# First loads from two queues, first half units over six PSUM banks, statistics spread

## The chip, the cores and the metric

The kernel runs on one core of one Trainium2 chip. The metric is the time of one execution on the device in microseconds; where several runs are given, their median.

## The reference

```python
def reference(A_x, A_w_r, A_w_i, B_x, B_w_gate, B_w_up, B_w_down):
    def _A_ref(x, w_r, w_i):
        X = rfft2(x.astype(float32), axes=(-2, -1))
        X = X * (w_r + 1j * w_i)
        return irfft2(X, s=(S, D), axes=(-2, -1)).astype(bfloat16)

    def _B_ref(x, w_gate, w_up, w_down):
        g = jnp.einsum("bsd,df->bsf", x, w_gate)
        u = jnp.einsum("bsd,df->bsf", x, w_up)
        h = _gelu(g) * u
        return jnp.einsum("bsf,fd->bsd", h, w_down)

    x = A_x
    xn = _layernorm(x, axis=-1)
    return x + _A_ref(xn, A_w_r, A_w_i) + _B_ref(xn, B_w_gate, B_w_up, B_w_down)
```

`x` is 1 x 2048 x 512, the weights of the gated part are 512 x 1792 (gate and up) and 1792 x 512 (down), all in bfloat16. The row x is normalized, goes through a spectral filter (a two-dimensional Fourier transform, a product, and back) and through a gated feed-forward layer, and the three are added.

## The kernel before, in words

The 2048 rows are 16 tiles `j` of 128 rows (row 16p + j is on partition p of tile j), and four blocks `b` of four tiles. Everything is issued in an order that is written out by hand from L699 on. `_Sched` keeps a list of instructions for each engine; an engine runs its list strictly in order and waits, before an instruction, on the semaphores of what it depends on. `_Ring` hands out PSUM banks in turn: the next user of a bank waits for the bank's last readers. Before the change there are three rings: three banks for the gate and up products (`ps_gu`), four for transposes and the spectral part (`ps_sp`), one for the down product (`ps_dn`).

Loads: ACT's queue issues `small` at L345, 224 KB that hold the identity (the first 128 columns), BM and CM. SP's queue issues all the rest in the order of L347 to L373: x tiles 0 to 3 one by one, the first piece of the gate and up weights (columns 0 to 255, called w0 here), the second piece (256 to 767, w1), x tiles 4 to 7, the third piece w2, x tiles 8 to 15, w3, the constants `fa` of the spectral part, the down weights `wd`. The pieces are cut by `WPIECES`, and a piece counts as loaded when both its transfers, gate and up, are there.

The start, L699 to L723: 18 warm-up matmuls on zeros run on the matmul engine (PE). DVE takes mean and variance of tiles 0 and 1 (`ln_stats`: L399 and L400), ACT a square root (L405), DVE a reciprocal (L409) and the normalized rows (`ln_apply`, L422). PE transposes them (L440): four transposes into each of two banks, copied to `xnT` by DVE (L446) and by ACT (L448). Then come six half units on the first 256 rows of block 0, one for each of six chunks `fc` of 128 weight columns. A half unit (`geglu_unit`) is four matmuls for the gate (from `wg_sb`) and four for up (`wu_sb`), all L495, 256 columns wide; ACT applies gelu (L507) and DVE multiplies into `hT` (L515). Chunks 0 and 1 need w0, chunks 2 to 5 need w1. Ahead of chunk 2, DVE normalizes tiles 2 and 3, whose statistics it took after the first copies, with the reciprocal root from GpSimd (POOL, `ln_rstd`, L414 and L415). After the six half units tiles 2 and 3 are transposed, and six more half units do the second 256 rows. In DVE's list the statistics of tiles 4 and 5 stand ahead of the first of these, those of tiles 6 and 7 ahead of the second.

From L746 on the units are full, 512 columns wide, beginning with chunk 6 of block 0. After it, DVE normalizes tiles 4 to 7, POOL starts the folds of the spectral part (L460, L461), one more unit follows, and tiles 4 to 7 are transposed (16 transposes). From there on the spectral part's stages (L567, L583, L614, L635, L661, L681) and the full and down units (L543) alternate on PE until the last four down units, which end the kernel.

Of the kernel before, what the change touches and what calls it, by code (L numbers as in the profile page):

```python
# [209 lines left out]

class _Ring:

    def __init__(self, nslots):
        self.n = nslots
        self.pos = 0
        self.readers = [[] for _ in range(nslots)]

    def alloc(self, n=1):
        while self.pos % n != 0:
            self.pos += 1  # L220
        base = self.pos % self.n
        self.pos += n
        deps = []
        for s in range(base, base + n):
            deps.extend(self.readers[s])
            self.readers[s] = []
        return base, deps
# [8 lines left out]
def bass_parallel_sum__spectral_gfnet__glu_gated_geglu__prompt_kernel(  # L236
# [21 lines left out]
    with ExitStack() as es:  # L258
# [49 lines left out]
        EM = eg[:, 0:NJ * P].rearrange("p (j q) -> p j q", j=NJ)  # L308
        G = eg[:, NJ * P:].rearrange("p (r k) -> p r k", r=4)

        ps_gu = es.enter_context(nc.psum_tensor("ps_gu", [P, 3 * 512], F32))
        ps_sp = es.enter_context(nc.psum_tensor("ps_sp", [P, 4 * 512], F32))
        ps_dn = es.enter_context(nc.psum_tensor("ps_dn", [P, 512], F32))
        ps_sp_bf = ps_sp[:, :].bitcast(BF16)

        def gu_bank(slot):
            return ps_gu[:, slot * 512:(slot + 1) * 512]

        def sp_bank(slot):
            return ps_sp[:, slot * 512:(slot + 1) * 512]  # L320

        def sp_pair(slot):
            return ps_sp[:, slot * 512:(slot + 2) * 512].rearrange("p (a c) -> p a c", a=2)[:, :, 0:NK]

        def sp_bank_bf(slot):
            return ps_sp_bf[:, slot * 1024:(slot + 1) * 1024]

        ring_gu = _Ring(3)
        ring_sp = _Ring(4)
        ring_dn = _Ring(1)  # L330

        streams = [("pe", 1), ("act", 1), ("dve", 1), ("pool", 1)]
        streams += [(n, 16) for n in ("x0", "x1", "x2", "x3", "xc1", "xc2", "xc3", "small", "fa", "eg", "wd", "wr", "wi",
                                      "w0", "w1", "w2", "w3", "dr0", "dr1", "perm1", "perm2_0", "perm2_1", "out")]
        for name, inc in streams:
            sem = es.enter_context(nc.semaphore("sem_" + name))
# [5 lines left out]
            return total(stream)  # L342


        ev_small = load("small", small[:], c_small.ap(), eng="act")  # L345
        ev_x = {}
        for j in range(4):  # L347
            ev_x[j] = load("x%d" % j, x_sb[:, j, :], xv[:, j, :])
# [2 lines left out]
        ev_w = {}  # L351
        spec = {}

        def load_w(i):
            a, b = WPIECES[i]
            for dst, src in ((wg_sb, B_w_gate), (wu_sb, B_w_up)):
                load("w%d" % i, dst[:, :, a:b], src[:, a:b].rearrange("(r p) f -> p r f", p=P))
            ev_w[i] = total("w%d" % i)

        def load_xc(m):  # L360
# [1 line left out]
            for j in range(4 * m, 4 * m + 4):  # L362
                ev_x[j] = ev

        load_w(0)
        load_w(1)
        load_xc(1)
        load_w(2)
        load_xc(2)
        load_xc(3)  # L370
        load_w(3)
        ev_fa = load("fa", fa[:], c_fa.ap())
        ev_wd = load("wd", wd_sb[:], wdv)  # L373
        d1 = nc.dram_tensor("stage_p", [NJ, P, 512], BF16).ap()
# [50 lines left out]
        ev_xnT = {}  # L425
        tr = {}

        def transposes(a, b):

            n = (b - a) * P  # L430
            evs = []
            for h in range(2):
                slot, bdeps = ring_sp.alloc(1)
                bank = sp_bank_bf(slot)[:, 0:2 * n].rearrange("p (r s) -> p r s", r=2)

                def f_tr(e, h=h, bank=bank):
                    ins = None
                    for r in range(2):
                        for j in range(a, b):
                            ins = e.transpose(bank[:, r, (j - a) * P:(j - a + 1) * P], xn[:, j, (2 * h + r) * P:(2 * h + r + 1) * P], ident)  # L440
                    return ins

                ev_t = sch.op("pe", f_tr, deps=[ev_small] + [ev_xn[j] for j in range(a, b)] + bdeps)
                dst = xnT[:, 2 * h:2 * h + 2, a * P:b * P]
                if h == 0:
                    ev = sch.op("dve", lambda e, dst=dst, bank=bank: e.tensor_copy(dst, bank), deps=[ev_t])  # L446
                else:
                    ev = sch.op("act", lambda e, dst=dst, bank=bank: e.activation(dst, bank, ACT.Copy), deps=[ev_t])  # L448
                ring_sp.add_reader(slot, ev)
                evs.append(ev)  # L450
            for j in range(a, b):
                ev_xnT[j] = evs
                tr[j] = ev_t
# [16 lines left out]
        def warm_up():  # L470

            ev = sch.op("dve", lambda e: e.memset(hT[1][:, 0, :], 0.0))

            def f(e):
                ins = None
                for i in range(NWARM):
                    ins = e.matmul(ps_dn[:, :], hT[1][:, 0, 0:P], hT[1][:, 0, :], start=True, stop=True)
                return ins

            hT_readers[1].append(sch.op("pe", f, deps=[ev]))  # L480

        def geglu_unit(b, fc, a=0, w=512):

            k = geg["k"]
            geg["k"] = k + 1
            s2 = k % NGG
            hb = b % 2
            evw = [ev_w[i] for i, (lo, hi) in enumerate(WPIECES) if lo < (fc + 1) * P and fc * P < hi]
            evx = [ev_xnT[4 * b + i] for i in range(a // P, (a + w) // P)]
            gslot, gdeps = ring_gu.alloc(1)  # L490

            def mm(e, wsb, slot, dcs=range(NDC)):
                ins = None
                for dc in dcs:
                    ins = e.matmul(gu_bank(slot)[:, 0:w], wsb[:, dc, fc * P:(fc + 1) * P], xnT[:, dc, b * 512 + a:b * 512 + a + w],  # L495
                                   start=(dc == 0), stop=(dc == NDC - 1))
                return ins

            if b == 0 and fc == 0:
                sch.op("pe", lambda e: mm(e, wg_sb, gslot, (0, 1)), deps=evw + [x[0] for x in evx] + gdeps)  # L500
                ev_gm = sch.op("pe", lambda e: mm(e, wg_sb, gslot, (2, 3)), deps=[x[1] for x in evx])
            else:
                ev_gm = sch.op("pe", lambda e: mm(e, wg_sb, gslot), deps=evw + evx + gdeps)
            uslot, udeps = ring_gu.alloc(1)
            ev_um = sch.op("pe", lambda e: mm(e, wu_sb, uslot), deps=udeps)
            gg = gg_sb[s2][:, 0:w]
            ev_gg = sch.op("act", lambda e: e.activation(gg, gu_bank(gslot)[:, 0:w], ACT.Gelu_apprx_tanh),  # L507
                           deps=[ev_gm] + gg_readers[s2])
            gg_readers[s2] = []
            ring_gu.add_reader(gslot, ev_gg)  # L510
            hdeps = []
            if fc == 0 and a == 0:
                hdeps = list(hT_readers[hb])
                hT_readers[hb] = []
            ev_h = sch.op("dve", lambda e: e.tensor_tensor(hT[hb][:, fc, a:a + w], gu_bank(uslot)[:, 0:w], gg, ALU.mult),  # L515
                          deps=[ev_um, ev_gg] + hdeps)
            ring_gu.add_reader(uslot, ev_h)
            gg_readers[s2].append(ev_h)
            ev_h_block.setdefault(b, []).append(ev_h)

# [8 lines left out]
        def down_unit(b, jj):  # L529
            hb = b % 2  # L530
            j = 4 * b + jj

            ring, bank = (ring_gu, gu_bank) if b == 3 else (ring_dn, lambda slot: ps_dn[:, :])
            parts = 2 if j == NJ - 1 else 1
            w = D // parts
            for h in range(parts):
# [168 lines left out]
        ln_recip(0, 2, ev_sq)  # L705
        ln_apply(0)
        ln_apply(1)
        transposes(0, 2)
        ln_stats(2)
        ln_stats(3)  # L710
        ln_rstd(2, 4)
        for fc in range(NHALF):
            if fc == 2:
                ln_apply(2)
                ln_apply(3)
            geglu_unit(0, fc, 0, 256)
        transposes(2, 4)
        for fc in range(NHALF):
            if fc in (0, 1):
                ln_stats(4 + 2 * fc)  # L720
                ln_stats(5 + 2 * fc)
            geglu_unit(0, fc, 256, 256)
        ln_rstd(4, 8)  # L723
        fillers = []
        for b in range(4):
# [22 lines left out]
            ln_apply(j)  # L748
        folds(0, [ev_xn[7]])
        filler()  # L750
        transposes(4, 8)
        folds(1)
        filler()
        for m in range(2, NDC + 2):
            for i in range(4):
                j = 4 * (m - 2) + i
                if m < NDC:
                    if i < 2:
                        ln_stats(4 * m + 2 * i)
                        ln_stats(4 * m + 2 * i + 1)  # L760
                    else:
                        ln_apply(4 * m + 2 * i - 4)
                        ln_apply(4 * m + 2 * i - 3)
                    if i == 1:
                        ln_rstd(4 * m, 4 * m + 4)
                filler()
                unit_d(j)
                if j >= 1:
                    unit_A(j - 1)
                if j == 1:  # L770
                    load_filter("wr", wr_sb, A_w_r)
                if j == 5:
                    load_filter("wi", wi_sb, A_w_i)
                if j == 9:
                    shuffle(0)
            if m < NDC:
                transposes(4 * m, 4 * m + 4)
                folds(m)
        filler()
        unit_A(NJ - 1)  # L780
# [70 lines left out]
```

## Time and profile before

| what | value |
|---|---|
| median of 3 runs | 196.79 us (196.22 to 196.89) |
| the profiled execution | 197.14 us, its span 195.4 us |
| busy share of the span | PE 96%, weight loads 53%, DVE 49%, ACT 46%, POOL 21% |
| chain that ended last | PE 89%, DVE 4%, DMA 4%, SP's queue 2% |
| read from HBM, written | 15.71 MB, 4.19 MB |
| DMA issues at the start, KB each, us from issue to landing | x tiles 0 to 3: 128.0, 3.5 (median); w0 gate: 256.0, 4.4; w0 up: 256.0, 5.5; small: 224.0, 3.0 |

The profile is one execution taken by the hardware profiler. The span runs from its first instruction to its last, so the execution's own time lies a little above it. An arrow in a line names what ended the idle time before an instruction. "PEld" is the weight load of the matmul engine, which overlaps matmuls.

### The profile page before, as it was taken

What the parts mean: (1) busy time and instruction counts of PE and PEld (TensorE: products, weight loads), DVE (VectorE), ACT (ScalarE), POOL (GpSimd) and SP (SyncE); (2) the same over time, 40 slices, a digit from 0 to 9 for tenths busy, and PEclk for the clock granted to TensorE, in tenths of its full rate; (3) what the DMA queues carried; (4) which work ended last, traced back from release to release, by engine and by line L of the source; (5) the groups of instructions that cost most, each with busy time, mean ns of one, the idle gap of its engine ahead of it and who ended that gap; (6) DMA issues with size and microseconds to landing.
All of it is one profiled execution on the core that took longest, in us unless ns stands there. A gap on an engine that the chain in (4) does not pass through costs nothing.

```text
span 195.4 us, 3030 instructions
## 1 busy us (share of the span) xinstructions
PE 187.5 (96%) x1120; PEld 103.8 (53%) x1120; DVE 95.2 (49%) x200; ACT 90.6 (46%) x167; POOL 40.2 (21%) x38
## 2 busy tenths in 40 slices
PE   7878999999999999999999999999999999999995
PEld 2465645555555554445555555544555555554453
DVE  2758469595322122445555455514454646465221
ACT  2534344776747462237546563633443635365000
POOL 0010259464530000000000000000134424444200
PEclk9999999999999999999999999999999999999999
DMA  4999950599996742900112111110001111110011
GB/s 143 323 370 375 374 185 2 128 182 198 253 197 154 207 142 83 325 25 18 51 46 56 49 50 51 48 51 20 2 27 61 50 54 43 41 54 0 11 46 54
DMA packets 25294, 22.20 MB, mean 114 GB/s; under 512 B 1472, under 2 KB 24512, under 8 KB 25152
## 3 DMA queue, kind: packets, MB, share of 16 engines
q1 hardware_dynamic: 25136, 21.78, 40.2%
q10 hardware_dynamic: 144, 0.23, 0.5%
q8 instruction: 9, 0.15, 0.3%
q14 instruction: 5, 0.04, 0.1%
HBM read 15.71 MB, written 4.19 MB: 102 GB/s over the span
## 4 chain that ended last, share of the span: by engine, by line
PE 89%; DVE 4%; DMA 4%; SPq 2%; issue 1%; ACT 0%; DVEq 0%
PE ps_gu L495 46%; PE ps_dn L543 19%; PE ps_gu L543 6%; DMA wu_sb<-in_B_w_up_dram 4%; PE ps_sp L567 4%; PE ps_sp L681 3%; PE ps_sp L661 2%; PE ps_sp L614 2%; PE ps_sp L636 2%; PE ps_sp L635 2%; PE ps_sp L583 2%; SPq L341 2%; PE ps_sp L440 1%; DVE hT L515 1%; DVE st L399 1%; DVE bufA L422 1%
## 5 line engine op out<-in xcount | busy, mean ns | idle before, releaser
L495 PE MATMUL ps_gu<-xnT,wg_sb 128*128 128x512 bf16 (+1 forms) x248 | 58.6, 358 | 3.3 <-DMA wu_sb<-in_B_w_up_dram 1.1
L495 PE MATMUL ps_gu<-xnT,wu_sb 128*128 128x512 bf16 (+1 forms) x248 | 58.5, 358 | 0.0
L515 DVE TENSOR_TENSOR hT<-ps_gu,gg 128x512 bf16<-128x512 f32 (+1 forms) x62 | 39.4, 637 | 35.0 <-PE ps_gu L495 34.3
L507 ACT ACTIVATE gg<-ps_gu 128x512 bf16<-128x512 f32 (+1 forms) x62 | 34.5, 557 | 27.9 <-PE ps_gu L495 27.8
L693 POOL TENSOR_TENSOR x_sb<-x_sb,bufC 128x512 bf16<-128x512 bf16 x16 | 18.4, 1151 | 108.8 <-DVE bufC L688 108.8
L543 PE MATMUL ps_dn<-wd_sb,hT 128*128 128x512 bf16 x168 | 38.2, 379 | 0.0
L495 PEld LDWEIGHTS ps_gu<-xnT,wu_sb 128*128 128x128 bf16 x248 | 24.3, 98 | 24.2
L495 PEld LDWEIGHTS ps_gu<-xnT,wg_sb 128*128 128x128 bf16 x248 | 23.5, 98 | 20.8 <-DMA wu_sb<-in_B_w_up_dram 2.4
L543 PEld LDWEIGHTS ps_dn<-wd_sb,hT 128*128 128x128 bf16 x168 | 16.4, 98 | 17.9
L549 DVE TENSOR_TENSOR x_sb<-ps_dn,x_sb 128x512 bf16<-128x512 f32 x12 | 8.3, 692 | 23.2 <-PE ps_dn L543 23.2
L575 ACT ACTIVATE X<-ps_sp 128x512 bf16<-128x512 f32 x16 | 11.9, 745 | 14.8 <-PE ps_sp L567 14.8
L641 ACT ACTIVATE Vp<-ps_sp 128x514 bf16<-128x514 f32 x16 | 9.6, 599 | 18.3 <-PE ps_sp L636 9.6
L666 ACT ACTIVATE bufA<-ps_sp 128x512 bf16<-128x512 f32 x16 | 9.6, 597 | 17.1 <-PE ps_sp L661 17.1
L622 DVE TENSOR_TENSOR M<-Xc,wr_sb 128x514 bf16<-128x514 bf16 x16 | 6.9, 428 | 14.7 <-ACT Xc L619 14.7
L543 PE MATMUL ps_gu<-wd_sb,hT 128*128 128x512 bf16 (+1 forms) x70 | 12.3, 337 | 0.3 <-DVE hT L515 0.3
L399 DVE BATCH_NORM_STATS2 st<-x_sb 128x6 f32<-128x512 bf16 x16 | 10.7, 672 | 2.6 <-DMA x_sb<-in_A_x_dram 2.6
L460 POOL TENSOR_TENSOR bufB<-xnT 128x1024 bf16<-128x1024 bf16 x4 | 8.5, 2124 | 15.0 <-DVE bufA L422 5.6
L619 ACT ACTIVATE Xc<-ps_sp 128x514 bf16<-128x514 f32 x16 | 9.5, 595 | 4.0 <-PE ps_sp L614 4.0
L686 DVE TENSOR_TENSOR bufC<-ps_sp,bufC 128x256 bf16<-128x256 f32 x16 | 6.8, 424 | 6.7 <-ACT bufC L685 6.7
L543 PEld LDWEIGHTS ps_gu<-wd_sb,hT 128*128 128x128 bf16 x70 | 6.8, 98 | 5.9 <-DVE hT L515 0.6
L681 PE MATMUL ps_sp<-fa,bufA 128*128 128x256 bf16 x64 | 9.6, 273 | 0.0
L567 PE MATMUL ps_sp<-fa,bufB 128*128 128x256 bf16 x64 | 9.6, 272 | 0.0
(42 smaller groups left out, 142.9 us busy)
## 6 DMA issues: line engine op xcount, KB each, us to landing
stage_p<-bufA SPq DMA_DIRECT2D x16, 128.0 KB, 5.2
bufC<-stage_p SPq DMA_DIRECT2D x4, 512.0 KB, 5.2
bufB<-Vp SPq DMA_DIRECT2D x64, 32.0 KB
out_dram<-x_sb SPq DMA_DIRECT2D x15, 128.0 KB, 1.8
wd_sb<-in_B_w_down_dram SPq DMA_DIRECT2D x1, 1792.0 KB, 14.4
wr_sb<-in_A_w_r_dram SPq DMA_DIRECT2D x6, 257.0 KB, 5.2
wi_sb<-in_A_w_i_dram SPq DMA_DIRECT2D x6, 257.0 KB, 8.0
wg_sb<-in_B_w_gate_dram SPq DMA_DIRECT2D x3, 512.0 KB, 7.7
```

The lines of the kernel that those rows point to most:

```text
L399: ev = sch.op("dve", lambda e: e.bn_stats(st[:, j, :], x_sb[:, j, :]), deps=[ev_x[j]])
L495: ins = e.matmul(gu_bank(slot)[:, 0:w], wsb[:, dc, fc * P:(fc + 1) * P], xnT[:, dc, b * 512 + a:b * 512 + a + w], start=(dc == 0), stop=(d ...
L507: ev_gg = sch.op("act", lambda e: e.activation(gg, gu_bank(gslot)[:, 0:w], ACT.Gelu_apprx_tanh), deps=[ev_gm] + gg_readers[s2])
L515: ev_h = sch.op("dve", lambda e: e.tensor_tensor(hT[hb][:, fc, a:a + w], gu_bank(uslot)[:, 0:w], gg, ALU.mult), deps=[ev_um, ev_gg] + hdeps)
L543: ins = e.matmul(bank(slot)[:, 0:w], hT[hb][:, fc, jj * P:(jj + 1) * P], wd_sb[:, fc, cs], start=(fc == 0), stop=(fc == NFC - 1))
L567: ins = e.matmul(bank, fold[:, r, j * P:(j + 1) * P], FD[:, r, :], start=(r % 2 == 0), stop=(r % 2 == 1))
L575: ev_X1[j] = sch.op("act", lambda e: e.activation(dst, src, ACT.Copy), deps=[ev_p, X1_readers[j % NX1]])
L619: ev_c = sch.op("act", lambda e: e.activation(Xc[s2][:], sp_pair(slot), ACT.Copy), deps=[ev_p] + Xc_readers[s2])
L641: ev_v = sch.op("act", lambda e: e.activation(Vp[s2][:], sp_pair(slot), ACT.Copy), deps=[ev_p] + Vp_readers[s2])
L666: ev_ZT[j] = sch.op("act", lambda e: e.activation(ZT[:, :, j, :], src, ACT.Copy), deps=[ev_p] + [spec["dr%d" % q] for q in range(2)])
L681: ins = e.matmul(bank[:, h:h + HD], ZT[:, ci, j, :], G[:, ci, :], start=(ci < 2), stop=(ci >= 2))
L693: ev_o = sch.op("pool", lambda e: e.tensor_tensor(x_sb[:, j, :], x_sb[:, j, :], rS[s2], ALU.add), deps=[a, b, ev_xn[j]] + ev_acc.get(j, []))
```

## The change

1. ACT's queue issues the identity alone (32 KB, a semaphore of its own), and behind it the two transfers of w0. SP's queue goes from the x tiles straight to w1. The rest of `small` is loaded by SP behind w3, ahead of `fa`.
2. The eight PSUM banks become one tensor with one list of readers, and a ring is a tuple of bank numbers. The three old rings keep their banks (0 to 2, 3 to 6, 7). Two new ones share them: `ring_first`, six banks (0, 1, 2, 7, 5, 6) for the twelve half units, and `ring_tr`, banks 3 and 4, for the transposes of tiles 2 and 3 and of tiles 4 to 7.
3. The first transposes (tiles 0 and 1) go to four banks, two transposes each (`per=1`), and four copies, by DVE and ACT in turn. The first half unit's four gate matmuls wait each for its own copy.
4. The transposes of tiles 2 and 3 move from behind the sixth half unit to behind the fourth.
5. The statistics of tiles 4 to 7 come one at a time, behind the first four half units of the second 256 rows, not two at a time ahead of the first two.

```diff
 class _Ring:
-    def __init__(self, nslots):
-        self.n = nslots
+    def __init__(self, banks, readers):
+        self.banks = banks
         self.pos = 0
-        self.readers = [[] for _ in range(nslots)]
+        self.readers = readers
     def alloc(self, n=1):
-        while self.pos % n != 0:
-            self.pos += 1
-        base = self.pos % self.n
+        self.pos = -(-self.pos // n) * n
+        base = self.banks[self.pos % len(self.banks)]
...
+        bank_readers = [[] for _ in range(8)]
+        ring_gu = _Ring((0, 1, 2), bank_readers)
+        ring_sp = _Ring((3, 4, 5, 6), bank_readers)
+        ring_dn = _Ring((7,), bank_readers)
+        ring_first = _Ring((0, 1, 2, 7, 5, 6), bank_readers)
+        ring_tr = _Ring((3, 4), bank_readers)
...
-        ev_small = load("small", small[:], c_small.ap(), eng="act")
+        ev_id = load("ident", small[:, 0:P], c_small.ap()[:, 0:P], eng="act")
...
-        load_w(0)
+        load_w(0, eng="act")
         load_w(1)
...
         load_w(3)
+        ev_small = load("small", small[:, P:], c_small.ap()[:, P:])
         ev_fa = load("fa", fa[:], c_fa.ap())
...
-        def transposes(a, b):
+        def transposes(a, b, ring, per=2):
...
-            for h in range(2):
-                slot, bdeps = ring_sp.alloc(1)
+            for h in range(NDC // per):
+                slot, bdeps = ring.alloc(1)
...
-                if h == 0:
+                if h % 2 == 0:
                     ev = sch.op("dve", lambda e, dst=dst, bank=bank: e.tensor_copy(dst, bank), deps=[ev_t])
                 else:
                     ev = sch.op("act", lambda e, dst=dst, bank=bank: e.activation(dst, bank, ACT.Copy), deps=[ev_t])
...
-            if b == 0 and fc == 0:
-                sch.op("pe", lambda e: mm(e, wg_sb, gslot, (0, 1)), deps=evw + [x[0] for x in evx] + gdeps)
-                ev_gm = sch.op("pe", lambda e: mm(e, wg_sb, gslot, (2, 3)), deps=[x[1] for x in evx])
+            if b == 0 and fc == 0 and a == 0:
+                for dc in range(NDC):
+                    ev_gm = sch.op("pe", lambda e, dc=dc: mm(e, wg_sb, gslot, (dc,)), deps=evw + [x[dc] for x in evx] + gdeps)
...
-        transposes(0, 2)
+        transposes(0, 2, ring_sp, 1)
         ln_stats(2)
         ln_stats(3)
         ln_rstd(2, 4)
         for fc in range(NHALF):
-            if fc == 2:
+            geglu_unit(0, fc, 0, 256, ring_first)
+            if fc == 1:
                 ln_apply(2)
                 ln_apply(3)
-            geglu_unit(0, fc, 0, 256)
-        transposes(2, 4)
+            if fc == 3:
+                transposes(2, 4, ring_tr)
         for fc in range(NHALF):
-            if fc in (0, 1):
-                ln_stats(4 + 2 * fc)
-                ln_stats(5 + 2 * fc)
-            geglu_unit(0, fc, 256, 256)
+            geglu_unit(0, fc, 256, 256, ring_first)
+            if fc < 4:
+                ln_stats(4 + fc)
         ln_rstd(4, 8)
...
-        transposes(4, 8)
+        transposes(4, 8, ring_tr)
```

More of the change, by code (lines that the diff above doesn't have):

```diff
@@ L309, in bass_parallel_sum__spectral_gfnet__glu_gated_geglu__prompt_kernel, with bank_of @@
         G = eg[:, NJ * P:].rearrange("p (r k) -> p r k", r=4)
[L311 to L320, printed above, removed]
+        ps = es.enter_context(nc.psum_tensor("ps", [P, 8 * 512], F32))
+        ps_bf = ps[:, :].bitcast(BF16)
+        def bank_of(slot):
+            return ps[:, slot * 512:(slot + 1) * 512]
+        gu_bank = sp_bank = bank_of
         def sp_pair(slot):
-            return ps_sp[:, slot * 512:(slot + 2) * 512].rearrange("p (a c) -> p a c", a=2)[:, :, 0:NK]
+            return ps[:, slot * 512:(slot + 2) * 512].rearrange("p (a c) -> p a c", a=2)[:, :, 0:NK]
         def sp_bank_bf(slot):
[L326 to L330, printed above, removed]
+            return ps_bf[:, slot * 1024:(slot + 1) * 1024]
+        bank_readers = [[] for _ in range(8)]
[4 more added lines that the diff above has]
+        ring_tr = _Ring((3, 4), bank_readers)
         streams = [("pe", 1), ("act", 1), ("dve", 1), ("pool", 1)]
-        streams += [(n, 16) for n in ("x0", "x1", "x2", "x3", "xc1", "xc2", "xc3", "small", "fa", "eg", "wd", "wr", "wi",
+        streams += [(n, 16) for n in ("x0", "x1", "x2", "x3", "xc1", "xc2", "xc3", "ident", "small", "fa", "eg", "wd", "wr", "wi",
                                       "w0", "w1", "w2", "w3", "dr0", "dr1", "perm1", "perm2_0", "perm2_1", "out")]
@@ L352, in bass_parallel_sum__spectral_gfnet__glu_gated_geglu__prompt_kernel, with load_w @@
         spec = {}
-        def load_w(i):
+        def load_w(i, eng="sp"):
             a, b = WPIECES[i]
             for dst, src in ((wg_sb, B_w_gate), (wu_sb, B_w_up)):
-                load("w%d" % i, dst[:, :, a:b], src[:, a:b].rearrange("(r p) f -> p r f", p=P))
+                load("w%d" % i, dst[:, :, a:b], src[:, a:b].rearrange("(r p) f -> p r f", p=P), eng=eng)
             ev_w[i] = total("w%d" % i)
@@ L426, in bass_parallel_sum__spectral_gfnet__glu_gated_geglu__prompt_kernel @@
         tr = {}
-        def transposes(a, b):
+        def transposes(a, b, ring, per=2):
             n = (b - a) * P
             evs = []
-            for h in range(2):
-                slot, bdeps = ring_sp.alloc(1)
-                bank = sp_bank_bf(slot)[:, 0:2 * n].rearrange("p (r s) -> p r s", r=2)
+            for h in range(NDC // per):
+                slot, bdeps = ring.alloc(1)
+                bank = sp_bank_bf(slot)[:, 0:per * n].rearrange("p (r s) -> p r s", r=per)
                 def f_tr(e, h=h, bank=bank):
                     ins = None
-                    for r in range(2):
+                    for r in range(per):
                         for j in range(a, b):
-                            ins = e.transpose(bank[:, r, (j - a) * P:(j - a + 1) * P], xn[:, j, (2 * h + r) * P:(2 * h + r + 1) * P], ident)
-                    return ins
-                ev_t = sch.op("pe", f_tr, deps=[ev_small] + [ev_xn[j] for j in range(a, b)] + bdeps)
-                dst = xnT[:, 2 * h:2 * h + 2, a * P:b * P]
-                if h == 0:
+                            ins = e.transpose(bank[:, r, (j - a) * P:(j - a + 1) * P],
+                                              xn[:, j, (per * h + r) * P:(per * h + r + 1) * P], ident)
+                    return ins
+                ev_t = sch.op("pe", f_tr, deps=[ev_id] + [ev_xn[j] for j in range(a, b)] + bdeps)
+                dst = xnT[:, per * h:per * h + per, a * P:b * P]
+                if h % 2 == 0:
                     ev = sch.op("dve", lambda e, dst=dst, bank=bank: e.tensor_copy(dst, bank), deps=[ev_t])
@@ L448, in transposes @@
                     ev = sch.op("act", lambda e, dst=dst, bank=bank: e.activation(dst, bank, ACT.Copy), deps=[ev_t])
-                ring_sp.add_reader(slot, ev)
+                ring.add_reader(slot, ev)
                 evs.append(ev)
@@ L476, in f, with geglu_unit @@
                 for i in range(NWARM):
-                    ins = e.matmul(ps_dn[:, :], hT[1][:, 0, 0:P], hT[1][:, 0, :], start=True, stop=True)
+                    ins = e.matmul(bank_of(7), hT[1][:, 0, 0:P], hT[1][:, 0, :], start=True, stop=True)
                 return ins
             hT_readers[1].append(sch.op("pe", f, deps=[ev]))
-        def geglu_unit(b, fc, a=0, w=512):
+        def geglu_unit(b, fc, a=0, w=512, ring=None):
             k = geg["k"]
@@ L487, in geglu_unit @@
             hb = b % 2
+            ring = ring or ring_gu
             evw = [ev_w[i] for i, (lo, hi) in enumerate(WPIECES) if lo < (fc + 1) * P and fc * P < hi]
             evx = [ev_xnT[4 * b + i] for i in range(a // P, (a + w) // P)]
-            gslot, gdeps = ring_gu.alloc(1)
+            gslot, gdeps = ring.alloc(1)
             def mm(e, wsb, slot, dcs=range(NDC)):
@@ L497, in mm @@
                 return ins
-            if b == 0 and fc == 0:
-                sch.op("pe", lambda e: mm(e, wg_sb, gslot, (0, 1)), deps=evw + [x[0] for x in evx] + gdeps)
-                ev_gm = sch.op("pe", lambda e: mm(e, wg_sb, gslot, (2, 3)), deps=[x[1] for x in evx])
+            if b == 0 and fc == 0 and a == 0:
+                for dc in range(NDC):
+                    ev_gm = sch.op("pe", lambda e, dc=dc: mm(e, wg_sb, gslot, (dc,)), deps=evw + [x[dc] for x in evx] + gdeps)
             else:
                 ev_gm = sch.op("pe", lambda e: mm(e, wg_sb, gslot), deps=evw + evx + gdeps)
-            uslot, udeps = ring_gu.alloc(1)
+            uslot, udeps = ring.alloc(1)
             ev_um = sch.op("pe", lambda e: mm(e, wu_sb, uslot), deps=udeps)
@@ L509, in geglu_unit @@
             gg_readers[s2] = []
-            ring_gu.add_reader(gslot, ev_gg)
+            ring.add_reader(gslot, ev_gg)
             hdeps = []
@@ L516, in geglu_unit @@
                           deps=[ev_um, ev_gg] + hdeps)
-            ring_gu.add_reader(uslot, ev_h)
+            ring.add_reader(uslot, ev_h)
             gg_readers[s2].append(ev_h)
@@ L531, in down_unit @@
             j = 4 * b + jj
-            ring, bank = (ring_gu, gu_bank) if b == 3 else (ring_dn, lambda slot: ps_dn[:, :])
+            ring, bank = (ring_gu if b == 3 else ring_dn), bank_of
             parts = 2 if j == NJ - 1 else 1
@@ L776, in bass_parallel_sum__spectral_gfnet__glu_gated_geglu__prompt_kernel @@
             if m < NDC:
-                transposes(4 * m, 4 * m + 4)
+                transposes(4 * m, 4 * m + 4, ring_sp)
                 folds(m)
```

## The prediction

> **What bounds the kernel now.** I read the busy line by slices first, then the waits of the matmul engine, then the opening of the timeline, and last the transfers.
>
> ```profile
> PE   7878999999999999999999999999999999999995
> ...
> PEclk9999999999999999999999999999999999999999
> DMA  4999950599996742900112111110001111110011
> ```
>
> Each digit is 4.9 us. PE is below nine tenths only in the first four slices and the last; its granted clock is full throughout. The waits of PE name what is missing (line, what was waited for, us in total, times, longest):
>
> ```profile
> PE ps_dn L477 <- DVE hT L472: 1.4, 1, 1.4
> PE ps_gu L495 <- DMA wu_sb<-in_B_w_up_dram: 1.1, 1, 1.1
> PE ps_gu L495 <- DVE hT L515: 0.9, 1, 0.9
> PE ps_gu L495 <- DVE st L399: 0.9, 1, 0.9
> PE ps_gu L495 <- DVE xnT L446: 0.5, 1, 0.5
> PE ps_sp L440 <- DVE bufA L422: 0.3, 1, 0.3
> PE ps_gu L543 <- DVE hT L515: 0.3, 1, 0.3
> ```
>
> That is every wait of PE over 195.4 us. All but the last (at 180.6 us, in the tail) lie before 26.6 us; from there to 180 us PE never waits. So a microsecond won at the start arrives at the end whole, as long as the later waits stay at zero. The timeline places them (start, duration, engine, line, what, idle before):
>
> ```profile
> 7.10 0.61 PE L440 MATMUL ps_sp<-small,bufA 128*128 128x128 bf16 x8
> ...
> 8.56 0.61 PE L495 MATMUL ps_gu<-xnT,wg_sb 128*128 128x256 bf16 x4 [0.85 <-DVE st L399]
> ...
> 11.56 0.61 PE L495 MATMUL ps_gu<-xnT,wg_sb 128*128 128x256 bf16 x4 [1.08 <-DMA wu_sb<-in_B_w_up_dram]
> ...
> 16.12 0.63 PE L495 MATMUL ps_gu<-xnT,wg_sb 128*128 128x256 bf16 x4 [0.45 <-DVE xnT L446]
> ...
> 19.99 0.61 PE L495 MATMUL ps_gu<-xnT,wg_sb 128*128 128x256 bf16 x4 [0.89 <-DVE hT L515]
> ...
> 22.62 1.03 PE L495 MATMUL ps_gu<-xnT,wg_sb 128*128 128x512 bf16 x4
> ...
> 26.59 1.07 PE L440 MATMUL ps_sp<-small,bufA 128*128 128x128 bf16 x16 [0.35 <-DVE bufA L422]
> ```
>
> The wait at 8.56 is put down to DVE, but the weight load beside it waited for the up-weights, whose first piece, issued at 3.05, landed 5.5 us later: 8.55. The transfers, by stretch (length, busy us of PE, PEld, DVE, ACT, POOL, clock, DMA share, GB/s):
>
> ```profile
> 3.00:4.00 1.00, 1.00 (x4) 0.33 (x3) 0.05 (x1) 0.00 (x0) 0.00 (x0) 1.00 0.88 301
> 4.00:5.00 1.00, 1.00 (x5) 0.40 (x4) 0.97 (x3) 0.00 (x0) 0.00 (x0) 1.00 0.50 122
> 5.00:6.00 1.00, 1.00 (x6) 0.46 (x5) 0.62 (x2) 0.30 (x1) 0.00 (x0) 1.00 0.78 235
> ...
> 10.00:11.00 1.00, 0.48 (x5) 0.19 (x2) 0.56 (x3) 0.38 (x1) 0.69 (x1) 1.00 1.07 399
> ```
>
> Behind the first x rows there is a hole of two microseconds at 122 and 235 GB/s; afterwards the engines run at about 370.
>
> **The loads.** SP issued four x rows (0.72 to 2.54), w0 (2.58 and 3.05) and w1 (3.61 and 4.22). Now ACT issues w0 behind the identity, so SP reaches w1 at 2.58, about 1.0 us sooner. The second w1 transfer now lands at 4.22 + 7.3 = 11.5 and releases PE at 11.56. The 192 KB of small that moves behind w3 no longer share the engines before it: 0.197 MB at 373 to 399 GB/s is 0.5 us. Filling the hole at 301 GB/s would move 0.245 MB more, another 0.65 us. So w1 lands between 11.5 (neither helps) and 10.35 (both in full); with two queues that also even out the engines 9.8 is the floor I allow. I take the bytes in full and half the hole: 10.7, released at 10.75, against 11.56.
>
> The Trainium skill, page "DMA: Bandwidth & Descriptors", section "Rules for kernel authors", says that spreading DMAs over issuing engines does not add bandwidth and only saves sequencer issue time. That speaks against any gain from the hole: by it w1 would land at 11.0 and the forecast would be 0.3 us slower. The rows above show the engines half idle from 4 to 5 us, so there bandwidth was not the limit; whether issue was, no row shows.
>
> ACT pays for this with two issues. On SP they took 0.43 and 0.52, so ACT's table load (1.28) moves from 1.17 to about 2.1 and ends near 3.4; its first real work, the square root, starts at 5.69. Cover: 2.3 us. Behind SP, the rest of small is one more issue ahead of fa (landed 23.5, first used at 31.0) and wd (landed 28.5, first used after 52): the order changes, the bytes do not, and both have microseconds to spare. BM and CM are first used by L614, far later still.
>
> Two transfers of 256 KB now run beside x0 to x3. x0 and x1 landed at 3.9 and 4.2; DVE reaches x1 at 4.78, and the normalized rows are done at 7.0, where the warm-up matmuls (1.44 + 5.64 = 7.08) hold PE anyway. So an earlier x gains nothing, and x1 may be 0.6 us late for nothing. With an equal share of the engines w0 lands at 7.5 to 8.2 (estimate: 1.08 MB of identity, x and w0 beside the first w1 bytes, at 300 GB/s from 2.3 us).
>
> **Four banks and the first unit.** The DVE copy of 128x512 takes 0.42 and of 128x1024 0.69, so of 128x256 about 0.28; ACT's are 0.60 and 1.02, so 0.39. Two transposes end near 7.37; DVE copies 7.41 to 7.69 and 7.72 to 8.0, ACT 7.5 to 7.9 and 7.9 to 8.3. Each first-unit matmul waits for its own quarter; the last starts near 8.35 and the first unit ends its issue at 8.9, the second at 9.8 (a half unit is eight matmuls, 0.875 us by the starts 11.56 and 12.44). Before that was 10.3. This 0.55 us is hidden: w1 (10.7) ends last there. It costs nothing and earns nothing unless w1 lands before 9.8. Four copies where there were two add 0.15 us to DVE and 0.2 to ACT, hidden in the same wait.
>
> **From w1 to the first full unit.** From 11.56 to 22.62 are 11.06 us. The work in it is ten half units, 8.75, and eight transposes, 0.44 (0.055 each, by the dense start of sixteen in 0.89): 9.19. So 1.87 us is stall, more than the idle rows add up to because the pipeline refills. It comes from three places. Transposes of rows 2 and 3 stood last before the half that reads them (0.45 and the refill); now they stand two half units (1.75 us) ahead, and the copies (0.42 and 0.60) fit. Their input is there: the stats, POOL's power and the applies end at about 11.7, PE asks at 10.75 + 1.75 = 12.5. Second, DVE did two stats pairs (0.88 each) ahead of each product L515, with three banks to wait in. Now a unit uses two of six banks, so its up bank returns three units later. I ran DVE's queue through: with the second half starting at T, the products end at T + 1.49, 2.87, 4.2, 5.57, 6.9 and 7.4, with one stats pair behind each of the first four. PE wants the banks of the first four back at T + 3.05, 3.92, 4.79 and 6.1: always later, by 0.5 to 1.6 us. So all 1.87 goes.
>
> Third, what is late next: DVE's backlog. The product of the first full unit is ready at T + 7.15 and DVE is free at 7.4, so the four applies and with them the transposes at 26.59 come 0.25 us later against PE than before; the wait of 0.35 there becomes 0.6. Bounds: 0 (gaps shrink) to 0.6 (each DVE instruction 0.05 longer).
>
> **Sum.** 0.81 + 1.87 - 0.25 = 2.43 us. The profiled execution took 197.14 with a span of 195.4, so 1.7 lies around the span; it stands 0.35 above the median of 196.79. I take the 2.4 off both: span 193.0, and against the median **194.4**.
>
> **Rivals.** *No earlier w1:* the engines were the limit and w1 lands at 11.5; only the stalls go, 1.87 - 0.25 = 1.6: 195.2. For it: DMA share above 1.0 from 6 us on. Against: 0.2 MB less stands before w1.
>
> *Earlier w1:* it lands by 9.8; then the first unit's 0.55 counts too, the applies at 11.7 hold the transposes for 0.15, and the gain is 0.81 + 1.87 + 0.95 - 0.15 - 0.25 = 3.2: 193.6. For it: the hole. Against: w1 alone is 1.05 MB, 2.8 us at 370.
>
> *A new wait takes it back, no change:* DVE has 1.37 us of work in each of four half units against PE's 0.875. If the products come behind so far that PE waits for a bank in each of the last three units, some 0.5 each, and the applies 0.6 late, 2.1 of the 2.7 is gone: 196.2. Against: the slack worked out above.
>
> *Slower:* issues on ACT block. SP's issues took 1.24 to 2.49 us where its queue was full. ACT executes in order, and the table load, the square root, the reciprocal, the applies and so the first transposes all stand behind. Two issues of 2.49 would end at 6.1, the square root would start at 7.4, and w1's cover leaves a loss of only 0.7. It decides from about 6.7 us for both together: then PE reaches its third unit at 13.2 and all of 2.4 is gone; at 4 us each it would be 198.1. Against: ACT's issue of small took 0.36, and SP's w0 0.43 and 0.52.
>
> **How the numbers follow.** Forecast 0.58, no earlier w1 0.15, earlier w1 0.12, no change 0.09, slower 0.06. The first three are all faster by over 0.5% (1 us, about what a measurement here can tell): 0.85; within 0.5% 0.09; slower by more 0.06. For the range, the forecast with w1 at 11.0 and 0.6 of backlog is 195.1; the spread of the times adds 0.3, as does the rival's 195.2, so 195.6 above; below, 193.6 less the spread: 193.2.
>
> **What would show it.** Right: the third unit's matmuls start at 10.4 to 11.1 still waiting for w1; no PE wait for L515 or L446 before 20 us; the first 512-wide matmul near 20.0 in place of 22.62; the 16 transposes near 24.2 with a wait of 0.3 to 0.9 for L422; nothing else waits until the tail. Wrong: a wait for ACT's L405 before 7 us, for L515 from 17 to 20 us, w1 at 11.5 or later, or a new wait of PE after 27 us, which would break the premise that the start's gain arrives whole.

## The result, and the profile after

The changed kernel took 194.03 us in the median of five runs (193.86 to 194.54); before it was 196.79. The ratio is 0.987, with an interval of 0.985 to 0.989. A second measurement of it, beside three experiments, gave 193.93 and a ratio of 0.9875 (0.986 to 0.989). The profiled execution took 194.54 with a span of 192.7; the one of before, 197.14 and 195.4.

The waits of PE over the whole execution after (line, what was waited for, us in total, times, longest):

```profile
PE ps L480 <- DVE hT L475: 1.4, 1, 1.4
PE ps L442 <- DVE bufA L424: 0.3, 1, 0.3
PE ps L547 <- DVE hT L519: 0.3, 1, 0.3
```

Of the seven waits of before, four are gone: w1, the banks behind the products, the copies to `xnT`, and the first one at the weights. What stays is the start of the warm-up, the wait for the normalized tiles 4 to 7, and the one in the tail. The timeline of PE places the steps (start, duration, engine, line, what, idle before):

```profile
1.43 6.94 PE L480 MATMUL ps<-hT 128*128 128x512 bf16 x18 [1.43 <-DVE hT L475]
...
8.21 0.61 PE L442 MATMUL ps<-small,bufA 128*128 128x128 bf16 x8
...
8.96 0.67 PE L499 MATMUL ps<-xnT,wg_sb 128*128 128x256 bf16 x4
...
10.78 0.60 PE L499 MATMUL ps<-xnT,wg_sb 128*128 128x256 bf16 x4
...
20.05 1.03 PE L499 MATMUL ps<-xnT,wg_sb 128*128 128x512 bf16 x4
...
24.02 1.07 PE L442 MATMUL ps<-small,bufA 128*128 128x128 bf16 x16 [0.35 <-DVE bufA L424]
```

The third half unit starts at 10.78 (11.56 before), the first full unit at 20.05 (22.62), the sixteen transposes at 24.02 (26.59). From there PE waits nowhere but in the tail, so the 2.57 us arrive at the end: the span is 2.7 shorter. In all fourteen traces of this document, whatever the start, the first full unit is followed by 172.7 us to the end of the span (172.65 to 172.78). But look at the first line: the same 18 warm-up matmuls took 6.94 us here and 5.64 before. They hold the first transposes, and through them the third half unit, which does not wait for w1. The normalized rows were there two microseconds before the transposes, as DVE's timeline shows:

```profile
5.37 0.73 DVE L424 TENSOR_SCALAR bufA<-x_sb,ag,rstd 128x512 bf16<-128x512 bf16 x2
```

The transfers, by stretch, and then the second w1 transfer (issued at 3.06, us to landing at the end of its line):

```profile
3.00:4.00 1.00, 1.00 (x4) 0.33 (x3) 0.86 (x3) 0.58 (x1) 0.00 (x0) 1.00 0.75 213
4.00:5.00 1.00, 1.00 (x4) 0.42 (x3) 0.77 (x3) 0.16 (x1) 0.00 (x0) 1.00 0.94 272
5.00:6.00 1.00, 1.00 (x4) 0.30 (x2) 0.79 (x3) 0.98 (x2) 0.00 (x0) 1.00 1.01 302
```

```profile
wu_sb<-in_B_w_up_dram SPq DMA_DIRECT2D x1, 512.0 KB, 7.1
```

The hole from 4 to 6 us (122 and 235 GB/s before) is mostly filled, while less was moved from 3 to 4 us (213, before 301), and w1 is complete at 3.06 + 7.1 = 10.1, not 11.5.

### The profile page after: what moved, and what is told of

It reads as the page before. It is cut to its first block, busy times and chain, and to the rows that moved or that the text cites. A ratio compares the mean times of both kernels' runs of the same rounds, so it can differ in the third digit from the quotient of the medians.

```text
span 192.7 us, 3034 instructions
## 1 busy us (share of the span) xinstructions
PE 188.0 (98%) x1120; PEld 104.4 (54%) x1120; DVE 95.1 (49%) x201; ACT 90.5 (47%) x168; POOL 40.2 (21%) x38
## 4 chain that ended last, share of the span: by engine, by line
PE 96%; DVE 2%; issue 0%
PE ps L499 49%; PE ps L547 25%; PE ps L571 4%; PE ps L480 4%; PE ps L685 3%; PE ps L665 2%; PE ps L618 2%; PE ps L640 2%; PE ps L639 2%; PE ps L442 2%; PE ps L587 2%; DVE hT L519 1%; DVE bufA L424 1%; DVE x_sb L553 0%; DVE xnT L449 0%
## 5 line engine op out<-in xcount | busy, mean ns | idle before, releaser
L499 PE MATMUL ps<-xnT,wg_sb 128*128 128x512 bf16 (+1 forms) x248 | 58.6, 358 | 0.1
L499 PE MATMUL ps<-xnT,wu_sb 128*128 128x512 bf16 (+1 forms) x248 | 58.5, 358 | 0.0
L519 DVE TENSOR_TENSOR hT<-ps,gg 128x512 bf16<-128x512 f32 (+1 forms) x62 | 39.3, 637 | 31.8 <-PE ps L499 30.3
L547 PE MATMUL ps<-wd_sb,hT 128*128 128x512 bf16 (+1 forms) x238 | 50.5, 366 | 0.3 <-DVE hT L519 0.3
L511 ACT ACTIVATE gg<-ps 128x512 bf16<-128x512 f32 (+1 forms) x62 | 34.5, 556 | 23.8 <-PE ps L499 23.2
L499 PEld LDWEIGHTS ps<-xnT,wu_sb 128*128 128x128 bf16 x248 | 24.3, 98 | 24.1
L547 PEld LDWEIGHTS ps<-wd_sb,hT 128*128 128x128 bf16 x238 | 23.2, 98 | 23.8 <-DVE hT L519 0.6
L499 PEld LDWEIGHTS ps<-xnT,wg_sb 128*128 128x128 bf16 x248 | 23.9, 98 | 16.8 <-issue 0.3
L579 ACT ACTIVATE X<-ps 128x512 bf16<-128x512 f32 x16 | 11.9, 746 | 14.7 <-PE ps L571 14.7
L670 ACT ACTIVATE bufA<-ps 128x512 bf16<-128x512 f32 x16 | 9.6, 597 | 17.1 <-PE ps L665 17.1
L591 ACT ACTIVATE bufA<-ps 128x512 bf16<-128x512 f32 x16 | 9.3, 584 | 0.5 <-PE ps L587 0.5
```

Source lines behind the costliest of these rows:

```text
L547: ins = e.matmul(bank(slot)[:, 0:w], hT[hb][:, fc, jj * P:(jj + 1) * P], wd_sb[:, fc, cs], start=(fc == 0), stop=(fc == NFC - 1))
L579: ev_X1[j] = sch.op("act", lambda e: e.activation(dst, src, ACT.Copy), deps=[ev_p, X1_readers[j % NX1]])
L670: ev_ZT[j] = sch.op("act", lambda e: e.activation(ZT[:, :, j, :], src, ACT.Copy), deps=[ev_p] + [spec["dr%d" % q] for q in range(2)])
```

## The experiments

The kernels were measured in three groups, each beside its own runs of the kernel before (medians 196.60, 196.41, 196.92; the first four rows of the table, the next four, the last four). Ratios to these are compared, since the medians of one kernel differ by up to half a microsecond between groups. 0.001 is 0.2 us, so a ratio's interval reaches about 0.3 us to each side, and a difference of two ratios is known to about half a microsecond.

| kernel | median us | ratio, interval |
|---|---|---|
| loads alone | 196.28 | 0.9985 (0.997 to 1.000) |
| all but the loads | 194.68 | 0.990 (0.989 to 0.992) |
| statistics in pairs | 194.66 | 0.991 (0.989 to 0.993) |
| three banks | 195.31 | 0.9935 (0.992 to 0.995) |
| the change again | 193.93 | 0.9875 (0.986 to 0.989) |
| 12 warm-up matmuls | 194.06 | 0.988 (0.9865 to 0.989) |
| first transposes in two banks | 194.14 | 0.989 (0.9875 to 0.9905) |
| transposes of 2 and 3 late | 195.05 | 0.993 (0.991 to 0.994) |
| w1 in two pieces, 12 warm-up | 192.91 | 0.980 (0.978 to 0.9825) |
| w1 in two pieces, 18 warm-up | 193.88 | 0.986 (0.984 to 0.988) |
| small split, w0 on SP | 194.83 | 0.990 (0.988 to 0.992) |
| small whole, w0 on ACT | 194.60 | 0.9885 (0.987 to 0.990) |

### The loads alone

```diff
 kernel before
-        ev_small = load("small", small[:], c_small.ap(), eng="act")
+        ev_id = load("ident", small[:, 0:P], c_small.ap()[:, 0:P], eng="act")
...
-        load_w(0)
+        load_w(0, eng="act")
...
         load_w(3)
+        ev_small = load("small", small[:, P:], c_small.ap()[:, P:])
...
```

> The kernel before with the loads alone changed: identity and w0 from ACT's queue, the rest of small behind w3; banks, transposes and statistics as before. Theory (the two parts add up): w1 lands near 10.1 in place of 11.5 and the third half unit starts 0.8 to 1.2 us sooner, while the stalls of the second half (1.9 us by starts) stay: 195.6 to 196.0. Rival (the later stalls set the time whatever the loads do, so the loads alone are worth nothing): 196.6 to 196.9. Rival (the loads are the whole gain): 194.0.

196.28, 0.3 us under the runs beside it, with an interval that reaches 1.000: all three were off. PE's waits and the lines behind them:

```profile
PE ps_gu L496 <- DVE hT L516: 0.9, 1, 0.9
PE ps_gu L496 <- DVE xnT L447: 0.8, 2, 0.5
```

```profile
10.56 0.60 PE L496 MATMUL ps_gu<-xnT,wg_sb 128*128 128x256 bf16 x4
...
21.70 1.03 PE L496 MATMUL ps_gu<-xnT,wg_sb 128*128 128x512 bf16 x4
```

In this trace no wait for w1 is left, the third half unit starts 1.0 us sooner, and from it to the first full unit are 11.14 us, as before (11.06): the later stalls stayed whole, as the theory had it. The span, 194.4, is 1.0 under the traced one of before; yet the timed runs moved by 0.3 only. The traced execution of before (197.14) was one of its longer ones, against 196.4 to 196.9 in the medians. The other runs of before were not traced, but an estimate can be had from the constant 172.7 us: the middle run of before in this group has a span of 194.8, so its first full unit starts near 22.1 and, if the 11.06 us ahead of that hold, its third half unit near 11.0, not at 11.56. By this estimate the gain read from the one trace was larger than a typical run has to give.

### All but the loads

```diff
 changed kernel
-        ev_id = load("ident", small[:, 0:P], c_small.ap()[:, 0:P], eng="act")
+        ev_id = ev_small = load("small", small[:], c_small.ap(), eng="act")
...
-        load_w(0, eng="act")
+        load_w(0)
...
-        ev_small = load("small", small[:, P:], c_small.ap()[:, P:])
```

> The changed kernel with the loads as before: all of small on ACT's queue, w0 on SP's. Theory: w1 lands at 11.5 again, the third half unit starts at 11.55 and not at 10.78, everything behind it stays stall-free: 194.8 to 195.1. Rival (banks and statistics are the whole gain): 194.0. Rival (the loads are the whole gain): 196.8.

194.68, 1.9 us under before and just below the range of the theory. Between the warm-up and the sixteen transposes PE waits once, where w1 is:

```profile
11.49 0.61 PE L498 MATMUL ps<-xnT,wg_sb 128*128 128x256 bf16 x4 [1.30 <-DMA wu_sb<-in_B_w_up_dram]
...
20.68 1.03 PE L498 MATMUL ps<-xnT,wg_sb 128*128 128x512 bf16 x4
```

From there to the first full unit are 9.19 us, the work that the prediction counted. So most of the gain is here: 1.9 of about 2.5 us, and the loads add some 0.6 on top, where the forecast gave them 0.8.

### Which part of the second half's gain

```diff
 statistics in pairs
         for fc in range(NHALF):
+            if fc in (0, 1):
+                ln_stats(4 + 2 * fc)
+                ln_stats(5 + 2 * fc)
             geglu_unit(0, fc, 256, 256, ring_first)
-            if fc < 4:
-                ln_stats(4 + fc)
...
 three banks
-            geglu_unit(0, fc, 0, 256, ring_first)
+            geglu_unit(0, fc, 0, 256, ring_gu)
...
-            geglu_unit(0, fc, 256, 256, ring_first)
+            geglu_unit(0, fc, 256, 256, ring_gu)
...
 transposes late
-            if fc == 3:
-                transposes(2, 4, ring_tr)
+        transposes(2, 4, ring_tr)
         for fc in range(NHALF):
             geglu_unit(0, fc, 256, 256, ring_first)
```

> The changed kernel with the statistics of tiles 4 to 7 two at a time ahead of the first two half units of the second 256 rows, as before; six banks stay. Theory: with six banks PE waits for the bank of the second product of that half, about 1.0 us, once: 194.8 to 195.2. Rival (six banks alone absorb it, the spread is worth nothing): 194.0. Rival (the spread is what counts, the banks nothing): the stall of before, 1.2 us, comes back in two places: 195.4.

> The changed kernel with the twelve first half units on the three banks of before; statistics spread. Theory: with three banks the gate of a unit waits for the product of the unit two before it, so PE goes at DVE's 1.37 us for four half units and not at 0.875: 1.2 us more, and 0.2 to 0.3 at the third half unit: 195.2 to 195.5. Rival (the spread alone absorbs it, six banks are worth nothing): 194.0.

> The changed kernel with the transposes of tiles 2 and 3 back behind the sixth half unit. Theory: PE waits for their copies, 0.45 idle and 0.15 of refill: 194.5 to 194.7. Rival (six banks and the spread statistics leave enough slack that the place does not matter): 194.0.

Statistics in pairs cost 0.6 to 0.7 us; three banks 1.2; the late place 1.0 to 1.1 (differences of the ratios to the change's 0.987 to 0.988, times 196.6; each is known to about half a microsecond). The second is as expected; the first is smaller (1.0 was expected) and the last larger (0.6). The traces give a finer measure: from the third half unit to the first full unit they take 0.67, 0.99 and 0.94 us more than the 9.19 of work. Where each wait sits, one line from each trace in that order:

```profile
18.37 0.61 PE L499 MATMUL ps<-xnT,wu_sb 128*128 128x256 bf16 x4 [0.50 <-DVE hT L519]
```

```profile
17.46 0.61 PE L499 MATMUL ps<-xnT,wg_sb 128*128 128x256 bf16 x4
...
18.60 0.61 PE L499 MATMUL ps<-xnT,wg_sb 128*128 128x256 bf16 x4
...
19.74 0.61 PE L499 MATMUL ps<-xnT,wg_sb 128*128 128x256 bf16 x4
```

```profile
15.19 0.60 PE L499 MATMUL ps<-xnT,wg_sb 128*128 128x256 bf16 x4 [0.78 <-ACT xnT L451]
```

The second trace is worth a look: no long idle time is listed, but the starts of the gate groups are 1.14 apart, not 0.875, because each unit waits for a product of the unit two before it. (1.14 us is what DVE needs for one statistics step and one product; the expectation had 1.37.) The idle rows hide most of that; the starts show it. In the third, PE waits for ACT's copy of the second bank (0.60 from 14.45), 0.78 us against 0.45 before. It costs more than the 0.6 of before, because there the first unit of this half began its gate on DVE's half of the copies, and the changed code waits for both (its finer waits hold only for `a == 0`). The three costs add to 2.9, more than the 1.9 us of all together, and by the traces to 2.6, so they overlap: with any one of the three missing, between a third and two thirds of the gain are lost.

### The start: four banks, the warm-up and w1

```diff
 two banks
-        transposes(0, 2, ring_sp, 1)
+        transposes(0, 2, ring_sp)
...
-                    ev_gm = sch.op("pe", lambda e, dc=dc: mm(e, wg_sb, gslot, (dc,)), deps=evw + [x[dc] for x in evx] + gdeps)
+                    ev_gm = sch.op("pe", lambda e, dc=dc: mm(e, wg_sb, gslot, (dc,)), deps=evw + [x[dc // 2] for x in evx] + gdeps)
...
 12 warm-up
-NWARM = 18
+NWARM = 12
```

> The changed kernel itself, beside the three that follow. 193.9 to 194.2 by the ratio 0.987; the profile should again show the third half unit between 9.8 and 10.8, by the later of w1's landing (10.1) and the end of the warm-up matmuls plus 2.4.

> The changed kernel with the first eight transposes in two banks, four each, and two copies, as before. Theory of the prediction (the four banks are hidden behind w1): 194.0. Rival (in the runs where the warm-up ends late nothing hides them, and the first unit is 0.3 later): 194.1 to 194.3.

> The changed kernel with 12 warm-up matmuls in place of 18. Theory: the normalized rows are done at 6.1, the warm-up holds the first transposes until 7.1 to 8.2; with 12 it ends between 5.6 and 6.6, PE reaches the end of w0's two units at 8.5 to 9.0 and then waits for w1 at about 10.1: the third half unit starts at 10.2 in every run, 0 to 0.6 sooner: 193.7 to 193.9. Rival (the warm-up is not what holds PE): 194.0, unchanged. Rival (with fewer warm-ups the clock stays low into the first units, matmuls of 256 columns at 0.21 and not 0.11): 195 or more.

The change again, a second trace of the same kernel:

```profile
1.43 5.99 PE L480 MATMUL ps<-hT 128*128 128x512 bf16 x18 [1.43 <-DVE hT L475]
...
10.22 0.61 PE L499 MATMUL ps<-xnT,wg_sb 128*128 128x256 bf16 x4 [0.24 <-DMA wu_sb<-in_B_w_up_dram]
```

Here the warm-up took 5.99 and w1 is what PE waits for. So two things end close to each other at the third half unit, and which is later changes from run to run: in the first trace PE came free 0.7 us behind w1, here 0.4 us ahead of it. With two banks the ratio is 0.989 against 0.9875, and the intervals overlap: the four banks are worth 0.3 us by the medians, which is not apart from the nothing that was forecast. With 12 warm-up matmuls nothing is won in the median either (0.988), for the reason that its trace gives:

```profile
7.37 0.61 PE L499 MATMUL ps<-xnT,wg_sb 128*128 128x256 bf16 x4 [0.29 <-DMA wu_sb<-in_B_w_up_dram]
...
10.35 0.61 PE L499 MATMUL ps<-xnT,wg_sb 128*128 128x256 bf16 x4 [1.06 <-DMA wu_sb<-in_B_w_up_dram]
```

The first unit starts at 7.37 and not at 8.0 to 9.0, and PE then waits a microsecond for w1. The matmuls of the first units run at the same 0.11 apart as before, so the clock did not suffer.

```diff
 w1 in two pieces, with NWARM 12 and 18
-        WPIECES = ((0, 256), (256, 768), (768, 1280), (1280, FF))
+        WPIECES = ((0, 256), (256, 512), (512, 768), (768, 1280), (1280, FF))
...
         load_w(1)
+        load_w(2)
         load_xc(1)
...
```

> The changed kernel with w1 cut in two pieces (columns 256 to 511, then 512 to 767) and 12 warm-up matmuls. Theory (two things end within half a microsecond of each other at the third half unit, the warm-up and w1, and each hides the other): with both out of the way the first w1 piece is there at about 8.7 and the third half unit starts at 9.1 and not at 10.2; the transposes of tiles 2 and 3 find their rows ready at 10.8 just in time: 192.7 to 193.2. Rival (something else holds the start, DVE or the transposes of tiles 2 and 3): 193.8 to 194.0.

> The changed kernel with w1 cut in two pieces and the 18 warm-up matmuls kept. Theory: the third half unit starts when the warm-up lets it, 9.1 to 10.8 depending on when the clock rises in a run: 193.5 to 193.9, little against 193.95. Rival (w1 alone was the bound): 192.9.

With 18 the ratio is 0.986, not apart from the change; with 12 it is 0.980, and 192.91 us is the fastest of all kernels here. The trace with 12:

```profile
1.44 4.79 PE L481 MATMUL ps<-hT 128*128 128x512 bf16 x12 [1.44 <-DVE hT L476]
...
9.02 0.61 PE L500 MATMUL ps<-xnT,wg_sb 128*128 128x256 bf16 x4
...
18.21 1.03 PE L500 MATMUL ps<-xnT,wg_sb 128*128 128x512 bf16 x4
```

The third half unit starts at 9.02. Either edit alone moved nothing that can be told; both together took another 0.7% off. That settles that each of warm-up and w1 hid the other.

### Bytes or queue

```diff
 small split, w0 on SP
-        load_w(0, eng="act")
+        load_w(0)
...
 small whole, w0 on ACT
-        ev_id = load("ident", small[:, 0:P], c_small.ap()[:, 0:P], eng="act")
+        ev_id = ev_small = load("small", small[:], c_small.ap(), eng="act")
...
-        ev_small = load("small", small[:, P:], c_small.ap()[:, P:])
```

> The changed kernel with w0 back on SP's queue; the identity alone stays ahead and the rest of small behind w3. Theory (192 KB fewer ahead are worth 0.5 us, the second queue the rest): w1 lands near 10.7, 194.2 to 194.5. Rival (only the second queue counts): w1 at 11.2 to 11.5, 194.7, as with the loads of before. Rival (only the bytes count): w1 at 10.1, 194.0.

> The changed kernel with all 224 KB of small ahead again on ACT's queue and w0 behind it there. Theory: w1 lands near 10.6, 194.0 to 194.4. Rival (only the second queue counts): w1 at 10.1, 194.0. Rival (only the bytes count): w1 at 11.2 to 11.5, 194.7.

By their traces w1 lands at 4.15 + 6.4 = 10.55 with the bytes alone taken away and at 3.06 + 7.8 = 10.86 with w0 alone moved, against 11.5 with neither and 10.1 with both. The times, 0.990 and 0.9885 against 0.990 and 0.987, point the same way for the queue and show nothing for the bytes, but their intervals overlap: the shares of the two are not settled. Both medians, 194.83 and 194.60, lie above what was expected of them; the runs of before beside them are the slowest of the three groups, 196.92. In the second, w0 itself lands late, and PE waits for it too:

```profile
8.78 0.61 PE L498 MATMUL ps<-xnT,wg_sb 128*128 128x256 bf16 x4 [0.59 <-DMA wu_sb<-in_B_w_up_dram]
```

## Why the prediction was right, step by step

**The time**, 194.4 against 194.03, and the mechanism held: every stall between w1 and the first full unit went, and the gain arrived whole. By the two traces: 0.78 at the third half unit (forecast 0.81); 11.06 - (20.05 - 10.78) = 1.79 between it and the first full unit (forecast 1.87); nothing for DVE's backlog (forecast a loss of 0.25), since the sixteen transposes come 3.97 after the first full unit, to the hundredth as before, behind the same wait of 0.35. The sum is 2.57, forecast 2.43.

**Mis-sized, and hidden by chance: the third half unit.** The forecast had it released by w1 at 10.75, with PE free at 9.8. In the trace w1 landed at 10.1, 0.6 us sooner, and PE came free at 10.78, 1.0 us later, because the warm-up ended at 8.37, not at 7.08. The step that failed is "the warm-up matmuls (1.44 + 5.64 = 7.08) hold PE anyway": the duration of one execution was taken for a constant. Over the twelve traces with 18 warm-up matmuls (before, after and ten experiments) it runs from 5.35 to 6.94. Two errors, 0.6 us the one way and 1.0 the other, met there, and that the start agrees to 0.03 us is luck. The second trace of the same kernel shows the forecast's picture, a wait for w1, at 10.22. In the trace of before the warm-up did not hold PE alone. In the trace after, the weight loads of the first transposes follow the last one of the warm-up by 0.12 us (7.87, 7.99). Before, they came 0.50 us behind it (4.75 + 1.82 = 6.57, 7.07) and 0.12 us behind the normalized rows (6.22 + 0.73 = 6.95):

```profile
7.07 0.46 PEld L440 LDWEIGHTS ps_sp<-small,bufA 128*128 128x128 bf16 x8 [0.49 <-issue]
```

So there earlier rows would have let PE go on up to 0.4 us sooner (an estimate, 0.50 - 0.12), against the forecast's "an earlier x gains nothing"; but the first weights (8.55) and w1 (11.5) would have hidden that.

**Mis-sized: the loads.** Taking them out of the change costs about 0.6 us, not 0.8, and alone they are worth 0.3, not apart from nothing, where the trace of before promised 0.8. w1 landed at 11.5 in both traces with the loads of before (before, and all but the loads), but the second was the longest of its six runs and the first stood above every median of its kernel. By the estimate above the third half unit of a typical run of before starts near 11.0; the same working puts that of the change near 10.2 (its span of 192.2, less 172.7 and 9.27). w0 landed at 1.68 + 5.3 = 7.0, sooner than the 7.5 to 8.2 of the forecast, which had no consequence.

**The rule weighed against the row.** The Trainium skill ("DMA: Bandwidth & Descriptors", "Rules for kernel authors") holds that spreading over queues adds no bandwidth. The rows here do not refute it. From 4 to 6 us the engines moved 272 and 302 GB/s after, 122 and 235 before; but the hole is also nearly filled with w0 on SP's queue and only the bytes of small taken away ("small split, w0 on SP"):

```profile
4.00:5.00 1.00, 1.00 (x4) 0.42 (x3) 0.74 (x2) 0.19 (x1) 0.00 (x0) 1.00 0.95 288
5.00:6.00 1.00, 1.00 (x4) 0.30 (x2) 0.82 (x3) 0.98 (x2) 0.00 (x0) 1.00 0.98 257
```

By 6 us 1.07 MB had been moved after and 0.95 before, and 1.05 in each of the two other traces with w0 on SP's queue; from 7 to 11 us the rate was 384 and 370 GB/s. What the second queue itself adds is open.

**The backlog.** The step that was mis-sized is DVE's 1.37 us for one statistics step and one product. In the trace after, products in that stretch start at 17.10, 18.23, 19.38 and 20.52, 1.14 apart, and the last of the half units' products ends at 20.52 + 0.74 = 21.26, before the first full unit's product starts at 21.98. So the bound of 0 was the value.

**The rivals.** The wait that was to take the place of the old one did not come: PE waits for no bank. ACT did not block: its two w0 issues took 0.53 each, and the square root, at 4.84, still waited 1.26 us for DVE. That SP's long issues of 1.24 to 2.49 us come from a full queue, as that rival has it, no row here shows; the rows show the durations.

## What to carry to other kernels

Where PE never waits after the start, look only at the start, and count a stall by the starts of equal pieces, not by the idle rows: the refill and short waits are not in these. Before removing the wait that is listed, ask what ends just before it; here warm-up and load ended within 0.7 us of each other, and only removing both paid. And take the durations of a start from more than one execution where an experiment allows it.

## What the runs showed of the hardware

The warm-up matmuls start 0.43 us apart until the matmul engine speeds up and about 0.21 afterwards, and that moment moves from run to run. Their weight loads show it, in the trace of before and then in that after, by the first line in which several come close together:

```profile
4.75 1.82 PEld L477 LDWEIGHTS ps_dn<-hT 128*128 128x128 bf16 x9 [0.20 <-issue]
```

```profile
7.34 0.53 PEld L480 LDWEIGHTS ps<-hT 128*128 128x128 bf16 x3 [0.24 <-issue]
```

The two traces of the changed kernel alone have it near 7.3 and near 5.4, with the same instructions. The granted clock reads 1.00 from 3 to 6 us before and after, so it does not show this; the spacing does. The Trainium skill ("TensorE: Matmul & The Clock Gate", Part 1) says that the slow phase is some 3.4 us and varies with a window that runs freely. The twelve traces with 18 warm-up matmuls have from 2.7 us (1.44 to about 4.2, with two banks) to 5.9 us (1.43 to 7.3): they agree that it varies, and here it is often well above 3.4. Over the runs of the change (193.58 to 194.54) it may be most of the spread; with 12 matmuls the four runs lie within 0.3 us, but that link was not shown by itself.
